# Moving the weight folds of a fused attention and gated-MLP kernel to 32x32 matrix tiles, and reordering its opening

## The chip, the core and the metric

The kernel runs on one core of a Trainium2 chip. A core has a matrix engine (TensorE, PE in the profile, with its weight loads listed as PEld), a vector engine (VectorE, DVE), an activation engine (ScalarE, ACT), a general engine (GpSimd, POOL) and a queue that issues most DMA transfers (SyncE, SP). Each engine works through its own list of instructions in order and waits on semaphores that the others raise. The metric is the device time of one execution in microseconds. The kernel before takes 2380.1 us (median of three runs, 2378.39 to 2380.84).

## The reference

`x` is 2048 tokens of 1024 values, normalised to `xn`. One branch is linear attention with 32 heads of 32 values and a learned feature map: a 32x32 matrix per head is applied to queries and keys before two softmaxes. The other branch is a SwiGLU MLP with 3584 hidden columns. Their product is added to `x`.

```python
qkv = (xn @ wqkv)                                   # q, k, v: 32 heads of 32
pq = einsum("bhsd,hdf->bhsf", q, w_phi)             # 32x32 per head
pk = einsum("bhsd,hdf->bhsf", k, w_phi)
phi_q = concat([softmax(pq), softmax(-pq)])         # the same for phi_k
kv = einsum("bhsf,bhsd->bhfd", phi_k, v);  z = sum_s phi_k
o = (phi_q @ kv) / (phi_q @ z + 1e-6)
s = o @ wo
h = silu(xn @ w1) * (xn @ w3);  g = silu(h @ w2)
out = x + s * g
```

## The kernel before

**Precision and products.** A matrix product in single precision is made as three products of values split into a high and a low part: `split` writes the high part as a cast on ACT (line 92) and the low part as a subtraction on DVE (line 93). Blocks are multiplied with a seven-product scheme (`ORDER`): each 2x2 block product takes seven products on sums of blocks, named A11, A12, S2, S1, S3, S4, A22 on the token side and B11, B21, T2, T1, T3, B22, T4 on the weight side. One such product is twelve matmuls of 128x512 and is here called a product; the gate and up projections of the MLP make 392 of them at line 598.

**The folds.** Since `w_phi` acts on each head of `q` and `k`, it can be multiplied into the key and query weights beforehand. Before, a fold is four f32 matmuls of 128x128 against `bd`, which holds the 32x32 matrices on the diagonal of 128x128 blocks (`fold`, line 247), a copy out of PSUM on ACT and a store to DRAM. There are 32 folds. Twelve of them (`FOLDS`) stand in the opening, twenty are placed as side work (`side_fold`).

**The opening.** The first 1024 tokens are loaded in two sets of four tiles. Each tile gets its mean and variance (`stats`, line 193, on DVE), the four deviations come from one square root on ACT (line 200) and a few small DVE operations (`rstd`), then `norm` (line 213), transposes on PE (`turn`, line 218), a copy out of PSUM on ACT (`raw_x`, line 223) and the split. All of this, in the order in which the code is written, is the order of each engine's list (`in_order`). The first four products are interleaved with it.

**The main loop and its side work.** `gate_up(step)` makes product number `step`, counted from 0; seven of them belong to one block of 128 hidden columns, `f`, and 28 such blocks to each half `tb` of the tokens. Around it stand the operands of later blocks and side work: normalising the other 1024 tokens (`side_x`), folds, the value and key weights (`side_kv`, which ends in 56 splits called `wkvo` and stores to `wkv_d`), `w2` (`side_w`). A function `room(step, cost)` gives DVE work a step: it adds the cost to a table of what each step already holds and moves on to the next step while the sum is over 2.55. Before, folds take no room.

**One hand-over of memory.** The side work's raw blocks come from the pool `xp` (14 buffers) and `bd` from `bdp`. At the first product of block `f = 25` (product 175) the code closes both and opens `spare` in the same place, and `fetch` (line 164, on SP) loads the second half's first operands, `op1A`, into it: eight DMAs. The code that issues the loads of `w1` and `w3` for the coming blocks (`b_load`, lines 256 and 257, tile `rw`, two buffers) puts them on the same SP list, and so are the stores of the hidden values (`h_d`) and of `wkvo`.

**The end.** After the last product of the MLP, `attend` (line 1336) and `out_half` (line 1351) work through 16 token tiles; `gate` (line 1053) applies the last silu on ACT.

Names that the later parts use: `bo` are split weight operands, `op0`/`op1` split token operands of the two halves, `u`, `h` hidden values, `wkv` raw blocks of `side_kv`, `consts` the statistics of the opening, `room_b` and `wr` the folds of the opening, `late_x` the second four token tiles.

Of the kernel before, what the change touches and what calls it, by code (L numbers as in the profile page):

```python
# [8 lines left out]
F = mybir.dt.float32  # L9
# [12 lines left out]
G = 8  # L22
# [7 lines left out]
def tile_kernel(ctx: ExitStack, tc: tile.TileContext, x, wkT, wqT, wv, wphi, wo, w1, w3, w2, out):  # L30
# [45 lines left out]
    wk_d = [[dram.tile([P, 512], F, name=f"wk_d{c}_{k}") for k in range(ND)] for c in range(2)]  # L76
    wq_d = [[dram.tile([P, 512], F, name=f"wq_d{c}_{k}") for k in range(ND)] for c in range(2)]
# [118 lines left out]
    def rstd(mv, sd=None):  # L196
# [3 lines left out]
        nc.scalar.activation(sd[:, 0], var, AF.Sqrt, bias=eps_t)  # L200
        yield sd
# [13 lines left out]
    def turn(half):  # L215
        pt = ps.tile([P, 4, P], F, name="pt", tag="tr", bufs=3)
# [33 lines left out]
    folds = [(wkT, k, c, wk_d[c][k]) for c in range(2) for k in range(ND)]  # L250
    folds += [(wqT, k, c, wq_d[c][k]) for c in range(2) for k in range(ND)]

    def b_load(f):

        rw = rwp.tile([P, 2, 2, 512], F, name="rw", tag="rw")
        nc.sync.dma_start(rw[:, 0], w1[f].rearrange("p (h k) n -> p h (k n)", h=2))
        nc.sync.dma_start(rw[:, 1], w3[f].rearrange("p (h k) n -> p h (k n)", h=2))
        return [rw[:, a, h] for a in range(2) for h in range(2)]

# [30 lines left out]
    phi_raw = flat(blk("phi")[:, :2]).rearrange("p (g f) -> p g f", f=DH)  # L290
    nc.sync.dma_start(phi_raw, wphi)
# [9 lines left out]
    for t in range(4):  # L301
        load_tile(t, quad("xt", F).rearrange("p u k t -> p u (k t)"))
        if t == 1:
            load_folds(2)
    rws = [b_load(0)]
    for t in range(4, 8):
        load_tile(t, late_x[:, t - 4])
    load_folds(4)
    rws.append(b_load(1))
# [76 lines left out]
    FIRST_PAIR = ((0, 0), (0, 1), (1, 0), (1, 1)) + tuple((f, j) for j in range(2, 7) for f in range(2))  # L386
# [107 lines left out]

    def side_fold(m, s0):
# [41 lines left out]
    for m in range(FOLDS, len(folds)):  # L537
        side_fold(m, FIRST_STEP + 48 + 11 * (m - FOLDS) // 2)
# [131 lines left out]
    for f in range(2):  # L670
        bos[0, f] = {}
        gens[0, f] = b_operands(rws.pop(0), bos[0, f], nc.gpsimd, held)
# [772 lines left out]
```

## Time and profile before

| | |
|---|---|
| runs, median (lowest, highest) | 2380.1 us (2378.39, 2380.84) |
| the profiled execution | 2381.62 us, its span 2379.8 us |
| PE busy | 2351.0 us, 99% |
| DVE, ACT, POOL busy | 1760.9, 910.1, 257.6 us |
| PE without work, 0 to 80 us | 15.9 us |
| PE without work, 80 to 2160 us | 7.6 us |
| PE without work, 2160 us to the end | 5.5 us |

The span is the time from the first to the last recorded instruction; the little that lies around it makes the time. A row of the timeline gives the start and the length in us, the engine, the line, the operation with its output and inputs, how many instructions were merged into the row, and in brackets how long the engine had been idle and who released it. A merged row's length is the time from its first start to its last end, and the last matmul's end reaches into the next row. An f32 matmul has two records in the trace. PEclk is the share of the full TensorE clock that the throttle granted.

### The profile page before, as it was taken

Reading aid. Unit: us, or ns where it says so; the run is one execution under the profiler, and the core shown is the slowest. Engines: PE = TensorE matmul, PEld = TensorE weight load, DVE = VectorE, ACT = ScalarE, POOL = GpSimd, SP = SyncE. Lnnn points to the kernel's source line nnn. Section 1 sums busy time; section 2 is a strip of 40 time slices with the busy share of each in tenths; the row PEclk is TensorE's granted clock in tenths of the full one; section 3 lists DMA queues with packets and bytes.
Section 4 is the critical chain, followed back from the end, with each engine's and each line's share of the span. In section 5 each row is a group of like instructions: output and inputs, shape, how many; then the busy total and the mean of one; then the engine's idle time right before and its main releaser. Section 6 shows DMA issues by size and latency. Waiting matters only on the chain.

```text
span 2379.8 us, 37194 instructions
## 1 busy us (share of the span) xinstructions
PE 2351.0 (99%) x14348; PEld 1934.9 (81%) x14348; DVE 1760.9 (74%) x2729; ACT 910.1 (38%) x1597; POOL 257.6 (11%) x243
## 2 busy tenths in 40 slices
PE   7999999999999999999999999999999999999999
PEld 6788888888888888888788888887888888887887
DVE  8877788765688888875566666777678888786775
ACT  6445454543444554543212222334433333352000
POOL 1000000000000000000000000331012222213562
PEclk9999999999999999999999999999999999999999
DMA  5446699985998888865977878986435653478763
GB/s 215 146 155 212 230 354 332 328 266 186 289 303 283 292 306 289 268 209 195 384 287 277 306 253 307 364 315 249 159 124 151 204 177 133 156 245 272 213 179 103
DMA packets 291472, 578.00 MB, mean 243 GB/s; under 512 B 24912, under 2 KB 140768, under 8 KB 288608
## 3 DMA queue, kind: packets, MB, share of 16 engines
q1 hardware_dynamic: 284960, 552.56, 68.5%
q10 hardware_dynamic: 6336, 23.07, 2.5%
q8 instruction: 113, 1.85, 0.3%
q14 instruction: 63, 0.52, 0.1%
HBM read 372.64 MB, written 202.91 MB: 242 GB/s over the span
## 4 chain that ended last, share of the span: by engine, by line
PE 93%; DVE 3%; DMA 2%; ACT 1%; SPq 1%; issue 0%; POOL 0%; DVEq 0%; ACTq 0%; POOLq 0%
PE bankb L598 24%; PE bankb L1199 13%; PE bankc L598 12%; PE pm L1351 8%; PE bankb L794 7%; PE bankc L1199 6%; PE banka L598 6%; PE bankc L794 3%; PE banka L1199 3%; PE bankb L861 3%; PE banka L794 2%; PE bankc L861 1%; PE po L1336 1%; PE pkv L779 1%; PE pw L247 1%; PE banka L861 1%
## 5 line engine op out<-in xcount | busy, mean ns | idle before, releaser
L93 DVE TENSOR_TENSOR bo<-rw,bo 128x512 fp32r<-128x512 f32 x336 | 230.9, 689 | 158.2 <-ACT bo L92 155.4
L1199 PE MATMUL bankb<-bo,as 128*128 128x512 f32 x960 | 235.2, 389 | 1.2 <-ACT acc L1205 1.2
L1199 PEld LDWEIGHTS bankb<-bo,as 128*128 128x128 f32 x960 | 180.2, 188 | 39.0 <-ACT acc L1205 1.6
L92 ACT CAST bo<-rw 128x512 fp32r<-128x512 f32 x336 | 206.5, 617 | 13.8 <-DMA w_d2B<-w2o 3.4
L598 PE MATMUL bankb<-op0S,bo 128*128 128x512 f32 x672 | 164.6, 394 | 1.9 <-ACT op0S L92 1.2
L598 PE MATMUL bankc<-op0S,bo 128*128 128x512 f32 x672 | 162.2, 391 | 0.0
L1351 PE MATMUL pm<-wos,oT 128*128 128x512 f32 x672 | 161.1, 394 | 0.9 <-DVE oT L1342 0.9
L598 PE MATMUL bankb<-op1S,bo 128*128 128x512 f32 x672 | 161.4, 389 | 0.6 <-ACT u L633 0.6
L598 PE MATMUL bankc<-op1S,bo 128*128 128x512 f32 x672 | 161.2, 389 | 0.0
L598 PE MATMUL bankb<-op0A,bo 128*128 128x512 f32 x672 | 159.7, 391 | 0.8 <-DVE bo L93 0.5
L771 POOL MEMSET ev<- 128x32 f32 x32 | 4.1, 129 | 1427.1 <-DMA xoA<-xo_d0A 1073.2
L1199 PE MATMUL bankc<-bo,as 128*128 128x512 f32 x624 | 158.4, 389 | 0.0
L598 PE MATMUL bankb<-op1A,bo 128*128 128x512 f32 x672 | 157.6, 390 | 0.0
L598 PEld LDWEIGHTS bankb<-op0S,bo 128*128 128x128 f32 x672 | 126.3, 190 | 29.0 <-ACT op0S L92 1.6
L1351 PEld LDWEIGHTS pm<-wos,oT 128*128 128x128 f32 x672 | 124.7, 188 | 29.5 <-DVE oT L1342 1.7
L598 PEld LDWEIGHTS bankb<-op1A,bo 128*128 128x128 f32 x672 | 125.9, 188 | 27.4 <-DVE u L641 1.3
L598 PEld LDWEIGHTS bankb<-op1S,bo 128*128 128x128 f32 x672 | 126.1, 188 | 27.1 <-ACT u L633 1.0
L598 PEld LDWEIGHTS bankc<-op1S,bo 128*128 128x128 f32 x672 | 126.1, 188 | 26.2
L598 PEld LDWEIGHTS bankb<-op0A,bo 128*128 128x128 f32 x672 | 125.2, 188 | 26.9 <-DVE bo L93 0.8
L598 PEld LDWEIGHTS bankc<-op0S,bo 128*128 128x128 f32 x672 | 125.4, 188 | 25.6
L1199 PEld LDWEIGHTS bankc<-bo,as 128*128 128x128 f32 x624 | 117.2, 188 | 24.4
L1213 DVE TENSOR_TENSOR acc<-bankb,acc 128x512 f32<-128x512 f32 x152 | 102.0, 685 | 31.1 <-PE bankb L1199 31.1
(262 smaller groups left out, 4343.8 us busy)
## 6 DMA issues: line engine op xcount, KB each, us to landing
rw<-in_w SPq DMA_DIRECT2D x112, 512.0 KB, 4.4
hr<-h_d SPq DMA_DIRECT2D x56, 512.0 KB, 4.8
h_d<-h SPq DMA_DIRECT2D x111, 256.0 KB, 5.4
xoS<-xo_d0S SPq DMA_DIRECT2D x44, 512.0 KB, 6.2
xoS<-xo_d1S SPq DMA_DIRECT2D x44, 512.0 KB, 6.1
xoA<-xo_d0A SPq DMA_DIRECT2D x33, 512.0 KB, 4.9
xoA<-xo_d1A SPq DMA_DIRECT2D x33, 512.0 KB, 4.4
e_d<-eq ACTq DMA_DIRECT2D x32, 512.0 KB, 6.3
```

The source lines that it names most:

```text
L92: nc.scalar.copy(hi, src)
L93: (by or nc.vector).tensor_sub(lo, src, hi.bitcast(F))
L247: nc.tensor.matmul(pw[:, g, :], wr[:, g], bd[:, 4 * c + g, :], start=True, stop=True)
L598: nc.tensor.matmul(bank[b], bos[tb, f][bn][:, w, k], ao[an][:, u, k], start=first and n == 0, stop=LAST[b] == an and n == 11, skip_group_c ...
L771: nc.gpsimd.memset(v[:, :, DH:], 1.0)
L779: nc.tensor.matmul(pkv[sl, m], e[:, m // 4, (m % 4) * P + 32 * h:(m % 4) * P + 32 * h + 32], v[:, 4 * (m % 4) + h], start=first and m == 0 ...
L794: nc.tensor.matmul(bank[b], xo[an][:, u, k], wb[bn][:, w, k], start=an in ("A11", "A12", "S1") and n == 0, stop=LAST[b] == an and n == 11, ...
L861: nc.tensor.matmul(bank[b], xo[an][:, u, k], wb[bn][:, w, k], start=an in ("A11", "A12", "S1") and n == 0, stop=LAST[b] == an and n == 11, ...
L1199: nc.tensor.matmul(bank[b], t[:, u, pos + k], bos[kb, bn, k][:, w], start=first and n == 0, stop=LAST[b] == an and n == 5, skip_group_chec ...
L1213: nc.vector.tensor_add(c, pb, c)
L1336: nc.tensor.matmul(po[32 * j:32 * j + 32, a, 64 * k:64 * k + 64], kvs[sl, j, c, k], et[sl, :, 4 * k + j], start=True, stop=True, skip_grou ...
L1351: nc.tensor.matmul(p, oTs[t, h][:, a, k], wos[c, 4 * h + k][:, b], start=n == 0, stop=n == 3 * ND - 1)
```

## The change

It has five parts. (1) The twenty folds of the side work become ten units. A unit takes the transposed weights of one group of four heads for all eight blocks of rows (two units: two groups, four blocks), 1024 values in each of 128 partitions, loaded into `bd`. It makes matmuls with the 32x32 matrix of a head as the stationary operand and 32 rows as the contraction: 16 of 256 columns, each in another 32x32 tile of the array, or 32 of 128 columns. They write four PSUM banks: three of the tag `tr` and one `banka`. DVE transposes each bank back in 32x32 blocks into `bd`, and one DMA stores it. Each pair of DVE transposes asks `room` for 0.7. (2) The four token tiles are loaded ahead of everything else, `w1` of two blocks ahead of both `w3`; twenty transposes of the raw tiles, whose results nobody reads, stand ahead of the first real ones. (3) The high and low parts of A11 and A12 are taken straight from PSUM, and the first four products run in the order A11 of blocks 0 and 1, then A12 of both. The folds of the opening stand behind the third product. (4) The order of the reads and statistics in the opening follows from that. (5) The silu of the last two tiles stands in the second and third turn of the last loop.

```diff
-    FIRST_PAIR = ((0, 0), (0, 1), (1, 0), (1, 1)) + ...
+    FIRST_PAIR = ((0, 0), (1, 0), (0, 1), (1, 1)) + ...
...
-    def rstd(mv, sd=None):
+    def rstd(mv, sd=None, between=None):
...
         nc.scalar.activation(sd[:, 0], var, AF.Sqrt, bias=eps_t)
+        if between:
+            between()
         yield sd
...
     for t in range(4):
         load_tile(t, quad("xt", F).rearrange("p u k t -> p u (k t)"))
-        if t == 1:
-            load_folds(2)
-    rws = [b_load(0)]
+    rws = [rwp.tile([P, 2, 2, 512], F, name="rw", tag="rw") for _ in range(2)]
+    b_part(rws[0], 0, 0)
+    phi_raw = early_z.rearrange("p (g f) -> p g f", f=DH)
+    nc.sync.dma_start(phi_raw, wphi)
+    load_folds(2)
+    b_part(rws[1], 1, 0)
     for t in range(4, 8):
         load_tile(t, late_x[:, t - 4])
+    for f in range(2):
+        b_part(rws[f], f, 1)
...
     def side_fold(m, s0):
-        wT, k, c, d = folds[m]
-        w = []
-        at(s0, lambda: w.append(load_w(wT, k, c)))
-        at(s0 + 5, lambda: w.append(flat(fold(w[0], c))), before)
-        at(s0 + 5, lambda: nc.scalar.copy(flat(w[0]), w[1]))
-        at(s0 + 7, lambda: nc.sync.dma_start(d, flat(w[0])))
+        w, banks = [flat(bd)], []
+        if m < 2:
+            gs_, nd = (4 + 2 * m, 5 + 2 * m), 4
+        else:
+            gs_, nd = (m - 2,), ND
...
+        def multiply():
+            banks.extend(ps.tile([P, 512], F, name="pf", tag="tr", bufs=3) for _ in range(3))
+            banks.append(ps.tile([P, 512], F, name="banka", bufs=BANKS["a"]))
+            for n, g in enumerate(gs_):
+                wn = w[0][:, 512 * n:512 * n + P * nd].rearrange("p (d k) -> p d k", d=nd)
+                for q in range(4):
+                    for j in (3, 0, 1, 2):
+                        sl = slice(32 * j, 32 * j + 32)
+                        nc.tensor.matmul(banks[j][32 * q:32 * q + 32, P * n:P * n + 32 * nd], phi_raw[sl, g], wn[sl, :, 32 * q:32 * q + 32],
+                                         start=True, stop=True, skip_group_check=True)
...
+        at(s0, multiply, before)
+        at_ = s0 - 1
+        for js in ((3, 0), (1, 2)):
+            at_ = room(at_ + 1, 0.7)
+            for j in js:
+                at(at_, lambda j=j: turn(j))
+        at(at_ + 2, store)
+        fold_free[0] = at_ + 4
...
-    for m in range(FOLDS, len(folds)):
-        side_fold(m, FIRST_STEP + 48 + 11 * (m - FOLDS) // 2)
+    for m, s0 in enumerate((52, 66, 87, 96, 108, 117, 129, 138, 150, 159)):
+        side_fold(m, s0)
...
+    nc.scalar.activation(sds[0][:, 1, :1], eps_t, AF.Sqrt)
+    warm = ps.tile([P, 512], F, name="banka", bufs=BANKS["a"])
+    for k in range(20):
+        nc.tensor.transpose(warm[:, :P], xs[2 + min(k // 8, 1)][k // 4 % 2][:, k % 4 * P:k % 4 * P + P], ident)
...
+    reads.append(gate_up(2))
+    first_folds(2)
+    first_copies(2)
+    stats(mvs[1], 0, xs[4])
+    stats(mvs[1], 1, xs[5])
+    reads[2]()
+    reads.append(gate_up(3))
     first_folds(4)
     load_folds(2)
     first_copies(2)
...
-    for j in range(2):
-        gate(len(pairs) - 1, j)
     prev = None
     for t in range(NT):
         p, last = out_half(t, 0), t + 1 == NT
         if t + 4 < NT:
             load_e(t + 4)
+        if 0 < t < 3:
+            gate(len(pairs) - 1, t - 1)
```

What this does to the lists of three engines is shown at three places. In these rows the number of a tile is kept, so that tiles of the same name can be told apart, and line numbers are those of the kernel that the row is from.

First, ACT in the opening, around the square root of the second four tiles (the row with `consts`). Before, the copies out of PSUM of the first two folds (`pw_473`, `pw_478`) stand ahead of it:

```order
L92 CAST op0A12_280<-xf_437 128x4x128
L333 COPY room_b_285<-pw_473 128x512
L333 COPY room_b_285<-pw_478 128x512
L200 ACTIVATE consts_274<-consts_274 128x4
L92 CAST bo_520<-rw_311 128x512
L92 CAST bo_523<-rw_311 128x512
L625 COPY h0_528<-bankb_439 128x512
```

Now four stand ahead of it. On PE the folds `pw_523` and `pw_528` follow the fourth product:

```order
L95 CAST bo_469<-rw_280 128x512
L682 COPY h0_472<-bankb_446 128x512
L343 COPY room_b_268<-pw_487 128x512
L343 COPY room_b_268<-pw_492 128x512
L343 COPY room_b_268<-pw_523 128x512
L343 COPY room_b_268<-pw_528 128x512
L203 ACTIVATE consts_257<-consts_257 128x4
L343 COPY wr_269<-pw_533 128x512
```

The square root has moved behind the copies of two folds that stand on PE behind the fourth product, where before it was behind folds that follow the second.

Second, DVE around the last of the 56 splits called `wkvo`. Before, it is `wkvo_4642`; the rows `L627` and `L641` around it read products 162 and 165, which belong to block 23:

```order
L93 TENSOR_TENSOR wkvo_4621<-wkv_4363,wkvo_4621 128x512
L627 TENSOR_TENSOR h0_4599<-banka_4601,h0_4599 128x512
L93 TENSOR_TENSOR bo_4639<-rw_4315,bo_4639 128x512
L93 TENSOR_TENSOR wkvo_4642<-wkv_4361,wkvo_4642 128x512
L93 TENSOR_TENSOR bo_4666<-rw_4479,bo_4666 128x512
L274 TENSOR_TENSOR rw_4479<-rw_4479,t2_4617 128x512
L93 TENSOR_TENSOR bo_4685<-rw_4479,bo_4685 128x512
L276 TENSOR_TENSOR rw_4479<-rw_4479,t2_4617 128x512
L641 TENSOR_TENSOR u1_4671<-bankb_4577,u1_4671 128x512
```

Now it is `wkvo_5123`; the rows `L698` and `L700` around it read products 179 and 180, which belong to block 25:

```order
L96 TENSOR_TENSOR wkvo_5103<-wkv_4808,wkvo_5103 128x512
L698 TENSOR_TENSOR u1_5085<-bankb_4992,u1_5085 128x512
L96 TENSOR_TENSOR bo_5120<-t2_5031,bo_5120 128x512
L96 TENSOR_TENSOR wkvo_5123<-wkv_4806,wkvo_5123 128x512
L700 TENSOR_TENSOR u0_5058<-bankc_5064,u0_5058 128x512
L701 TENSOR_TENSOR h0_5013<-h0_5013,u0_5058 128x512
```

The last split has moved two blocks down the list, past the point at which the code closes `xp`.

Third, the SP list around the loads of `op1A` into the memory of `xp`. Before, all stores of `wkvo` stand ahead of them, the last of them ten rows above the first row shown:

```order
L256 DMA rw<-in_w 128x1024
L257 DMA rw<-in_w 128x1024
L501 DMA wq_d_7_153<-wr 128x512
L164 DMA op1A_4882<-xo_d1A_94 128x8x128 x4
L164 DMA op1A_4887<-xo_d1A_95 128x8x128 x4
L556 DMA h_d_6_63<-h_4753 128x4x128
L256 DMA rw<-in_w 128x1024
L257 DMA rw<-in_w 128x1024
```

Now seven of these stores follow, two of them ahead of the next `rw`:

```order
L454 DMA wkv_d2T_121<-wkvo 256x1x512
L167 DMA op1A_4982<-xo_d1A_94 128x8x128 x4
L167 DMA op1A_4987<-xo_d1A_95 128x8x128 x4
L454 DMA wkv_d2B_115<-wkvo 256x1x512
L454 DMA wkv_d2B_116<-wkvo 256x1x512
L613 DMA h_d_6_63<-h_4839 128x4x128
L265 DMA rw<-in_w 128x1024 x2
L454 DMA wkv_d2T_117<-wkvo 256x1x512
L454 DMA wkv_d2T_118<-wkvo 256x1x512
```

The first of the four loads into `op1A_4982` waits for a semaphore of DVE that is raised by the split `wkvo_5123`; before, the first load waits for PE and for earlier DMAs.

More of the change, by code (lines that the diff above doesn't have):

```diff
@@ L700, in tile_kernel @@
     held.clear()
-    for t in range(1, 4):
+    for t in range(2, 4):
         stats(mvs[1], t, xs[4 + t])
@@ L704, in tile_kernel @@
     next(r1)
-    next(gens[0, 1])
-    next(gens[0, 1])
-    for do in held:
-        do()
-    reads[0]()
     first_copies(2)
-    reads[1]()
     load_folds(2)
@@ L732, in tile_kernel @@
     first_copies(2)
-    reads[3]()
     for f in range(2):
```

100 lines of the change are left out of this document (70 added, 30 removed).

## The prediction

> **What bounds the kernel now.** I read the page first, then busy time by stretches, then who PE waits for, and last the timeline of the places that the change touches. The page and the stretches (busy us of PE, PEld, DVE, ACT, POOL, then granted clock, DMA share, GB/s):
>
> ```profile
> span 2379.8 us, 37194 instructions
> PE 2351.0 (99%) x14348; PEld 1934.9 (81%) x14348; DVE 1760.9 (74%) x2729; ACT 910.1 (38%) x1597; POOL 257.6 (11%) x243
> ```
>
> ```profile
> 0.00:80.00 80.00, 64.06 (x330) 53.48 (x331) 68.71 (x129) 47.55 (x88) 8.38 (x16) 0.96 0.56 206
> 80.00:2160.00 2080.00, 2072.40 (x11159) 1709.32 (x11158) 1543.58 (x2434) 840.78 (x1475) 144.75 (x149) 1.00 0.73 250
> ```
>
> PE is the bound: it stands still for 16 us in the opening and 8 us in the 2080 us behind it. So a microsecond of PE work taken from the middle is a microsecond gained, and a wait that PE takes on there is lost in full. In the opening DVE is the busier of the two, 69 of 80 us. There a gain for PE counts only as far as DVE's list, and what feeds it, gets shorter.
>
> **The opening.** The rows that carry it:
>
> ```profile
> 9.79 1.29 DVE L193 BATCH_NORM_STATS2 st<-xt 128x6 f32<-128x512 f32 x2 [1.91 <-DMA xt<-in_x]
> 12.51 0.21 DVE L194 BATCH_NORM_AGGREGATE consts<-st 128x2 f32<-128x12 f32 x1
> 14.09 3.74 DVE L213 TENSOR_SCALAR xt<-xt,consts 128x512 f32<-128x512 f32 x8
> 17.75 1.28 DVE L93 TENSOR_TENSOR bo<-rw,bo 128x512 fp32r<-128x512 f32 x2
> 20.71 2.05 ACT L223 COPY xf<-pt 128x512 f32<-128x512 f32 x4
> 21.76 3.00 PE L598 MATMUL bankb<-op0A,bo 128*128 128x512 f32 x12
> 31.47 0.30 ACT L200 ACTIVATE consts<-consts 128x4 f32<-128x4 f32 x1 [0.60 <-DVE consts L194]
> 35.41 3.74 DVE L213 TENSOR_SCALAR late_x<-late_x,consts 128x512 f32<-128x512 f32 x8
> 47.86 6.13 PE L598 MATMUL bankb<-op0S,bo 128*128 128x512 f32 x24
> ```
>
> DVE lost 1.91 us on the third tile of x, which stood behind fold loads. With x first, four statistics of 1.45 us (1.29 and 0.21, overlapping a little) follow each other, and end near 10.5 instead of 12.7. The added split between the square root and the reciprocal (a cast of about 0.57, half of a pair of 1.14, and a subtraction of 0.64) takes back 1.1: the norms start near 13.0 instead of 14.1. High parts straight from PSUM let the first product begin near 16.5 and end near 19.5, five us earlier than now. But four products and their operands are not the end of the opening; the second four tiles are. Following DVE's list from 13.0: norms 1.9, four low parts 2.5, one weight split 0.6, norms 1.9, another split 0.6 gives 20.5; the A12 low parts wait half a us for their transposes and end at 23.5. The next split needs a cast that ACT has behind four A12 casts, a copy and four raw copies (2.05 for four): DVE stands for about 2 us, to 25.6. Two statistics bring 28.5, and only then comes the addition that empties the one `banka`, so the fourth product starts at 29.8 and ends at 32.5. Behind it are the folds whose copies stand ahead of the square root on ACT: it runs near 35, where DVE has its last statistics at 32.7, and the late norms start near 36.3 instead of 35.4. One addition of 0.6 now stands ahead of the sums. So the first S2 product comes at about 49.1 instead of 47.9: the five us are gone before 48.
>
> The clock pulls the other way:
>
> ```profile
> 11.00:14.30 3.30, 0.02 (x1) 0.00 (x0) 2.69 (x11) 1.79 (x5) 0.00 (x0) 1.00 1.03 421
> 14.30:17.70 3.40, 3.01 (x14) 3.01 (x15) 3.40 (x8) 1.58 (x4) 0.00 (x0) 0.50 1.02 414
> 17.70:21.00 3.30, 1.75 (x16) 1.47 (x14) 3.04 (x6) 3.28 (x7) 0.00 (x0) 1.00 1.06 413
> 62.10:65.50 3.40, 3.40 (x9) 2.62 (x10) 3.40 (x7) 1.10 (x3) 0.00 (x0) 0.50 0.32 133
> 65.50:69.00 3.50, 3.50 (x17) 2.90 (x16) 3.50 (x7) 3.50 (x8) 0.00 (x0) 1.00 0.00 0
> ```
>
> An idle stretch is followed by 3.4 us at half clock, which costs up to 1.7 us of PE work. The second such loss (at 62) may or may not fall on the changed kernel: between +1.2 with it and -0.8 without it I take +0.5, with -3 to +3 as ends. The twenty added transposes run while PE has nothing else; their cover is the wait for x, and they cost nothing. The Trainium skill (TensorE: Matmul & The Clock Gate, Part 4) says that transposes do not count as PE activity for the clock; by that the twenty would leave the first real transposes at half clock, some 1 us more in the sum. The trace speaks against it: the stretch 14.3 to 17.7 holds transposes alone, and the clock is full right behind it.
>
> **The folds.** A fold in the side work, and the nearest rows for a unit:
>
> ```profile
> 229.53 1.05 PE L247 MATMUL pw<-bd,wr 128*128 128x128 f32 x8
> 230.34 2.98 PE L598 MATMUL bankb<-op0S,bo 128*128 128x512 f32 x12
> 2172.29 0.86 PE L1336 MATMUL po<-acc,kvs 64*32 64x64 f32 x64
> 2173.08 0.98 PE L1351 MATMUL pm<-late,oT 128*128 128x512 f32 x3
> L1123 PE MATMUL us<-early_z,consts x2: 377/377/377, 2043.2 to 2043.4; 128*128 128x256 f32 x2
> 2170.07 2.37 DVE L1179 STREAM_TRANSPOSE acc<-acc 128x1024 f32<-128x1024 f32 x2
> ```
>
> From start to next start a fold takes 0.81 us, so twenty are 16.2 us, all on PE's path. The `po` rows show 32 small f32 matmuls (64 records) in 8 tiles of the array in 0.79 us, 0.025 each. One f32 matmul with 256 columns streams for about 0.4 us (the two records of `us` start 0.2 apart), so 64 columns take 0.1, and 32 of them one after another 3.2: eight tiles overlapped four times. For a unit (16 of 256 columns, or as many columns in all) that gives 16 x 0.4 / 4 = 1.6 as the upper end. The lower end is issue alone with one stream on its tail, 16 x 0.025 + 0.2 = 0.6. I take 0.9, nearer the lower end, since in `po` issue, not streaming, seems to have set the pace. Ten units: 9.0, a gain of 7.2 (0.2 to 10). The Trainium skill (TensorE: Matmul & The Clock Gate, Part 3) gives a speedup of 10.6 for 16 such tiles; by it a unit would stream for an estimated 0.6 us, the gain would be 10 and the sum 6. No run here shows 16 tiles.
>
> The twenty fold copies leave ACT, which is idle 60% of the time: nothing. DVE gets 40 transposes of 256 columns (0.3 each by the row of 1024 columns) and as much in the two narrow units, 12 us, with a quarter of its time free; a unit holds `banka` and all three `tr` banks until then. I book 0.5 for PE (0 to 2).
>
> **What the units push aside.** `room` now gives 20 slots of 0.7 to the folds, and the 56 `wkvo` splits move down DVE's list, the last from among the reads of products 162 to 165 to just ahead of that of product 180. The code closes `xp` at product 175. The load of `op1A` into its memory must wait for that split, and it is SP that waits. Behind it stand stores and `rw`, the weights of block 27. The rows of this place now:
>
> ```profile
> 512.55 0.69 DVE L93 TENSOR_TENSOR wkvo<-wkv,wkvo 128x512 fp32r<-128x512 f32 x1
> 538.12 11.90 SPq L164 DMA_DIRECT2D op1A<-xo_d1A  x8
> 550.11 2.27 SPq L556 DMA_DIRECT2D h_d<-h  x1
> 553.22 0.45 SPq L257 DMA_DIRECT2D rw<-in_w  x1
> 559.86 0.69 DVE L643 TENSOR_TENSOR u<-bankc,u 128x512 f32<-128x512 f32 x1 [1.43 <-PE bankc L598]
> 567.05 0.68 DVE L128 TENSOR_TENSOR rw<-rw 128x512 f32<-128x512 f32 x1
> 570.74 0.59 ACT L633 COPY u<-bankb 128x512 f32<-128x512 f32 x1 [0.50 <-PE bankb L598]
> 573.26 2.88 PE L598 MATMUL bankb<-op0S,bo 128*128 128x512 f32 x12
> ```
>
> ```profile
> rw<-in_w SPq DMA_DIRECT2D x2, 512.0 KB, 5.3
> op1A<-xo_d1A SPq DMA_DIRECT2D x8, 512.0 KB, 6.9
> 541.00:550.00 9.00, 9.00 (x42) 7.44 (x41) 5.67 (x9) 2.21 (x4) 0.00 (x0) 1.00 0.98 287
> ```
>
> Today 25 us lie between the last split (513.2) and the first load (538.1). The read at 559.86 is that of product 180; the split now comes about there, at 560 on today's clock, so SP stands some 22 us longer. From the first load to the landing of the second `rw` (553.22 and 5.3 us) took 20.4 us; two `wkvo` stores of 512 KB more are 2.5 us at the 421 GB/s of the opening's row: `rw` lands near 583. DVE wants it at 567.05. DVE then stands, behind it an addition that ACT's silu needs, behind that the copy at 570.74 which frees the bank for product 186, due at 573.26. From the sum at 567.05 to the end of that copy are 4.3 us: product 186 starts near 587, a stall of 14 us. If all 6.6 MB moved at those 421 GB/s, instead of 287 GB/s for `op1A`, `rw` would land near 578 and the stall be 9; with 287 for all of it, 16 to 17. I take 13.5, nearest to the transfers as they ran here (9 to 17). Such an idle stretch of PE ends at half clock: 1.7 more (0 to 3.4).
>
> **The last silus.**
>
> ```profile
> 2166.57 0.59 ACT L1341 CAST oT<-po 128x512 fp32r<-128x512 f32 x1 [0.27 <-PE po L1336]
> 2167.05 2.01 ACT L1053 ACTIVATE acc<-acc 128x1024 f32<-128x1024 f32 x2
> 2173.18 0.59 ACT L1341 CAST oT<-po 128x512 fp32r<-128x512 f32 x1 [4.12 <-PE po L1336]
> ```
>
> Nobody waits behind them: ACT idles for 4.12 us afterwards. Moving them is worth 0.
>
> **The sum.** +0.5 (opening) - 7.2 (folds) + 0.5 (DVE) + 13.5 (stall) + 1.7 (clock) + 0 = +9.0 us. The profiled execution took 2381.6 us, 1.5 above the median 2380.1, and would become 2390.6; for the median that is 2389.
>
> **The rivals.**
> *The block is hidden.* If the split came five products earlier, or the waiting load did not hold up those behind it, `rw` would be in time. For it speaks that every `rw` now lands 8 us or more before its sum (558.5 against 567.05). Against it: SP issues in order, and the lists put `rw` behind the load. Then the sum is 9.0 - 15.2 = -6.2: 2374, faster. It decides at a split done before 544 on today's clock, that is 567 less 23.
> *The stall is short and the units cheap.* 9 us of stall, 0.6 a unit: 9.0 - 4.5 - 3 = +1.5, 2381.6, the same. For it speaks the rate of 421 GB/s elsewhere; against it the 287 for this very load.
> *The tiles do not overlap.* A unit streams 16 x 0.4 = 6.4 us, ten 64 instead of 9: 2444. `po` speaks against it, but its streams are four times shorter.
>
> **How the numbers follow.** My forecast 0.73, the hidden block 0.09, the short stall 0.12, no overlap 0.06. A change under 0.2% (4.8 us) can't be told from none: slower above 2384.9, faster below 2375.3. Some of the forecast's own spread falls in the middle; that gives faster 0.09, same 0.14, slower 0.77. The range leaves out no overlap and the hidden block: its lower end 2377 lies just under a stall of 9 with units at 0.6 and the opening at -3 (9.0 - 4.5 - 3 - 3.5 = -2, so 2378); its upper end 2398 is stall 17 with units at 1.3 and 1.5 lost in the opening (9 + 3.5 + 4 + 1 = 17.5).
>
> **What would show it.** Each unit takes 0.6 to 1.6 us on PE between two products. The first product starts near 16.5, the late norms after 35, the square root of the late tiles behind a fold's copy. Near 570 to 585 PE stands 9 to 17 us, the chain of releasers going through ACT and DVE to the DMA of `rw`, and SP's own longest wait, over 20 us, is ahead of `op1A`. I am wrong if PE runs through there, if a unit takes over 2 us, or if the first S2 product starts before 46.

## The result and the profile after

| | before | changed |
|---|---|---|
| median of four runs | 2379.24 us | 2389.74 us |
| lowest, highest | 2378.26, 2380.84 | 2389.33, 2394.62 |
| profiled execution, its span | 2381.62, 2379.8 us | 2389.33, 2387.5 us |

The ratio is 1.0048 (95% interval 1.0031 to 1.0066): slower by about half a percent, where the forecast was 2389. The rows of the changed kernel that answer to those shown of before, first the page, then the stretches (busy us of PE, PEld, DVE, ACT, POOL; clock, DMA share, GB/s), then who waited longest on PE and on SP's queue:

```profile
span 2387.5 us, 37640 instructions
PE 2347.3 (98%) x14592; PEld 1924.1 (81%) x14592; DVE 1774.7 (74%) x2777; ACT 898.5 (38%) x1577; POOL 257.4 (11%) x243
```

```profile
0.00:80.00 80.00, 65.83 (x346) 55.62 (x347) 66.66 (x126) 46.49 (x87) 8.77 (x16) 0.98 0.55 202
80.00:2160.00 2080.00, 2059.76 (x11351) 1689.65 (x11350) 1554.55 (x2478) 825.47 (x1449) 143.56 (x148) 1.00 0.73 249
569.20:586.30 17.10, 5.89 (x14) 4.63 (x15) 5.72 (x9) 4.24 (x8) 0.00 (x0) 0.50 1.06 377
```

```profile
PE bankb L655 <- ACT u L690: 14.0, 1, 14.0
```

```profile
SPq L167 <- DVE wkvo L96: 24.3, 1, 24.3
```

PE has less to do than before (2347.3 against 2351.0 us) and takes longer. From 80 to 2160 us it stands still for 20.2 us instead of 7.6. One wait makes up 14.0 of them, and SP has a wait of 24.3 us that it did not have. Line numbers have moved: products are now L655, splits L95 and L96, the sum of `rw` L131, the load of `op1A` L167, that of `rw` L265, the square root L203, fold copies L343, the unit's matmuls L532.

The place of the stall, in the timeline of the changed kernel:

```profile
553.53 0.69 DVE L96 TENSOR_TENSOR wkvo<-wkv,wkvo 128x512 fp32r<-128x512 f32 x1 [1.79 <-ACT wkvo L95]
554.25 10.67 SPq L167 DMA_DIRECT2D op1A<-xo_d1A  x8
568.17 1.88 SPq L265 DMA_DIRECT2D rw<-in_w  x2
576.69 0.69 DVE L131 TENSOR_TENSOR rw<-rw 128x512 f32<-128x512 f32 x1 [14.35 <-DMA rw<-in_w]
578.74 0.63 ACT L688 ACTIVATE h<-h 128x512 f32<-128x512 f32 x1 [17.13 <-DVE h L684]
580.41 5.49 PE L655 MATMUL bankb<-op0S,bo 128*128 128x512 f32 x12 [14.03 <-ACT u L690]
585.70 3.21 PE L655 MATMUL bankc<-op0S,bo 128*128 128x512 f32 x12
```

It is read from below. Product 186 waits for ACT's copy of `u`, which stands behind the silu, which waits for DVE, which waits for `rw`. That load is issued at 568.17, behind the eight loads of `op1A`, and the first of these is issued at 554.25, 0.03 us after the end of the last `wkvo` split. The products are 5.49 and 3.21 us long where 2.88 is usual: PE is at half clock until 586.3.

The opening, in the same view:

```profile
17.30 3.29 PE L655 MATMUL bankb<-op0A,bo 128*128 128x512 f32 x12 [0.68 <-ACT op0A L738]
30.35 3.00 PE L655 MATMUL banka<-op0A,bo 128*128 128x512 f32 x12 [0.73 <-ACT room_b L343]
35.65 0.30 ACT L203 ACTIVATE consts<-consts 128x4 f32<-128x4 f32 x1
35.98 0.18 DVE L207 RECIPROCAL consts<-consts 128x4 f32<-128x4 f32 x1 [2.96 <-ACT consts L203]
49.71 0.50 PE L655 MATMUL bankb<-op0S,bo 128*128 128x512 f32 x1
```

The first product comes 4.5 us earlier than before and the fourth 9.4 (39.74 before), but the first S2 product 1.85 us later.

Where the 7.7 us between the two profiled spans come from, by the starts of the 392 products in both traces: the opening +1.0 (constant from product 11 to 51), folds and units -8.8, four small waits for DVE +0.7, the stall +14.2, half clock behind it +2.9, a wait of before at 650 us that is gone -0.9. That is +9.1 at the end of the MLP. The stages behind it give 1.5 back. The medians differ by 10.5 us, 2.8 more than these two executions.

### The profile page after: what moved, and what is told of

The parts are those of the page before. It is cut to its first block, busy times and chain, and to the rows that moved or that the text cites. A ratio compares the mean times of both kernels' runs of the same rounds, so it can differ in the third digit from the quotient of the medians.

```text
span 2387.5 us, 37640 instructions
## 1 busy us (share of the span) xinstructions
PE 2347.3 (98%) x14592; PEld 1924.1 (81%) x14592; DVE 1774.7 (74%) x2777; ACT 898.5 (38%) x1577; POOL 257.4 (11%) x243
## 4 chain that ended last, share of the span: by engine, by line
PE 94%; DVE 2%; DMA 2%; SPq 1%; ACT 0%; issue 0%; POOL 0%; DVEq 0%; ACTq 0%; POOLq 0%
PE bankb L655 25%; PE bankb L1280 13%; PE bankc L655 12%; PE pm L1432 8%; PE bankb L875 7%; PE bankc L1280 6%; PE banka L655 6%; PE bankb L942 4%; PE bankc L875 3%; PE banka L1280 3%; PE bankc L942 2%; PE banka L875 2%; PE po L1417 1%; PE banka L942 1%; PE pkv L860 1%; DMA op2T<-wkv_d1T 1%
## 5 line engine op out<-in xcount | busy, mean ns | idle before, releaser
L96 DVE TENSOR_TENSOR bo<-rw,bo 128x512 fp32r<-128x512 f32 x336 | 230.8, 688 | 153.6 <-ACT bo L95 153.2
L95 ACT CAST bo<-rw 128x512 fp32r<-128x512 f32 x336 | 206.7, 618 | 17.6 <-DMA w_d2B<-w2o 3.1
L655 PE MATMUL bankb<-op0S,bo 128*128 128x512 f32 x672 | 166.5, 398 | 14.8 <-ACT u L690 14.0
L655 PE MATMUL bankc<-op0S,bo 128*128 128x512 f32 x672 | 163.6, 392 | 0.3 <-DVE op0S L96 0.3
L655 PEld LDWEIGHTS bankb<-op0S,bo 128*128 128x128 f32 x672 | 128.4, 192 | 42.8 <-ACT u L690 14.4
L655 PE MATMUL bankb<-op1S,bo 128*128 128x512 f32 x672 | 161.2, 389 | 0.0
L655 PE MATMUL bankc<-op1S,bo 128*128 128x512 f32 x672 | 161.2, 389 | 0.0
L655 PE MATMUL bankb<-op0A,bo 128*128 128x512 f32 x672 | 159.2, 391 | 0.7 <-ACT op0A L738 0.7
L655 PE MATMUL bankb<-op1A,bo 128*128 128x512 f32 x672 | 157.6, 390 | 0.0
L655 PEld LDWEIGHTS bankc<-op0S,bo 128*128 128x128 f32 x672 | 125.4, 188 | 30.1 <-issue 2.9
L655 PEld LDWEIGHTS bankb<-op1A,bo 128*128 128x128 f32 x672 | 125.9, 188 | 27.4 <-DVE u L698 1.3
L655 PEld LDWEIGHTS bankb<-op0A,bo 128*128 128x128 f32 x672 | 125.2, 188 | 27.9 <-ACT op0A L738 0.9
L655 PEld LDWEIGHTS bankc<-op1S,bo 128*128 128x128 f32 x672 | 126.1, 188 | 26.2
L655 PEld LDWEIGHTS bankb<-op1S,bo 128*128 128x128 f32 x672 | 126.1, 188 | 26.2
```

Source lines behind the costliest of these rows:

```text
L95: nc.scalar.copy(hi, src)
L96: (by or nc.vector).tensor_sub(lo, src, hi.bitcast(F))
L655: nc.tensor.matmul(bank[b], bos[tb, f][bn][:, w, k], ao[an][:, u, k], start=first and n == 0, stop=LAST[b] == an and n == 11, skip_group_c ...
```

## The experiments

All are compared with the kernel before, run beside them; its median was between 2380.2 and 2381.2 us.

### Is it the reservations that make the stall?

Two rivals: the twenty `room` reservations, which only move DVE's list, or the units themselves. One run takes the reservations out of the changed kernel:

```diff
-            at_ = room(at_ + 1, 0.7)
+            at_ = at_ + 1
```

> The changed kernel, its units unchanged, but they reserve no room in DVE's list: the last wkvo split goes back to where it stood before the change. Theory (the reservations push the splits, op1A waits for the last one on SP, and rw of block 27 stands behind it): PE's 14.2 us stall ahead of product 186 and the 2.9 us of half clock behind it go, 2389.7 - 17.1 = 2372.6 us; SP's longest wait is no longer at op1A. Rival (the units themselves, their matmuls, transposes, loads or stores, make SP or DVE late): the stall stays, 2389 to 2390 us.

Another puts them alone into the kernel before:

```diff
         side_fold(m, FIRST_STEP + 48 + 11 * (m - FOLDS) // 2)
+    for s0 in (52, 66, 87, 96, 108, 117, 129, 138, 150, 159):
+        at_ = s0 - 1
+        for _ in range(2):
+            at_ = room(at_ + 1, 0.7)
```

> The kernel before, with its own folds and opening, but with the twenty reservations of 0.7 in the planner's table at the units' steps, and not one instruction added: only the order of DVE's list changes. Theory: the last wkvo split lands at the reads of products 179 to 180 again, so the stall of some 14 us and the 2.9 us of half clock come alone, 2379.2 + 17 = 2396 us. Rival (the units cause the stall): no change, 2379 us.

Without them: 2375.6 us, ratio 0.998 (0.997 to 0.9989). They alone: 2392.4 us, ratio 1.0054 (1.0039 to 1.0069). So the stall comes and goes with twenty entries in a table, with not one instruction added. The timeline of the kernel before with the reservations:

```profile
557.43 0.68 DVE L93 TENSOR_TENSOR wkvo<-wkv,wkvo 128x512 fp32r<-128x512 f32 x1
558.14 10.16 SPq L164 DMA_DIRECT2D op1A<-xo_d1A  x8
579.88 0.69 DVE L128 TENSOR_TENSOR rw<-rw 128x512 f32<-128x512 f32 x1 [9.97 <-DMA rw<-in_w]
583.60 5.19 PE L602 MATMUL bankb<-op0S,bo 128*128 128x512 f32 x12 [9.64 <-ACT u L637]
```

The stall is 9.6 us and not 14. Here `op1A` goes out behind the last split but one (557.43 and 0.68 make 558.11), 3.7 us ahead of the end of the last one (561.8); in the changed kernel it waited for the last. From the first load to the sum of `rw` it takes 21.7 us, against 22.4 there. The two differences make up the 4.4 us by which the stall is shorter.

### Is it SP's queue, or a late weight for another reason?

The changed kernel with its reservations, but the loads of `op1A` issued at product 178, behind `rw` of block 27:

```diff
-            for m in range(2):
-                early.update(fetch(tb + 1, m))
+            if tb:
+                for m in range(2):
+                    early.update(fetch(tb + 1, m))
         for late in load_at.get(step, ()):
             rws.append(b_load(late[1]))
+        if (tb, f, j) == (0, NF - 3, 3):
+            for m in range(2):
+                early.update(fetch(tb + 1, m))
```

> The changed kernel with its reservations, so that the wkvo splits are as late as in it, but the two loads into the memory of xp (op1A and its neighbour) are issued at product 178, behind the load of rw of block 27, instead of at product 175. Theory (SP issues in order, and rw is late only because it stands behind the waiting load): rw lands in time, the stall goes, 2372.6 us, though SP still waits for the split. Rival (rw is late because DVE's or the DMA engines' work has grown, not for its place behind op1A): 2389 to 2390 us.

2374.6 us, ratio 0.9977 (0.9968 to 0.9987). The split is as late as in the changed kernel, SP waits for it (6.0 us), and nobody minds:

```profile
546.55 0.81 SPq L265 DMA_DIRECT2D rw<-in_w  x2
552.69 0.68 DVE L96 TENSOR_TENSOR wkvo<-wkv,wkvo 128x512 fp32r<-128x512 f32 x1
553.40 10.33 SPq L167 DMA_DIRECT2D op1A<-xo_d1A  x8
561.04 0.68 DVE L131 TENSOR_TENSOR rw<-rw 128x512 f32<-128x512 f32 x1
```

`rw` goes out 6.9 us ahead of `op1A` and its sum has no wait. So the order on SP is the link. Both this run and the one without reservations stay 2 to 3 us above the 2372.6 expected. Their traces gain 15.6 us on the changed kernel at the end of the MLP, not 17.1: the one without reservations meets new waits of 0.46 us at 357 and of 1.17 at 599, and this one keeps the DVE waits and had an opening 1.0 us longer.

### What are the units worth, and does their order matter?

The kernel before with the units alone, no reservations, its own opening and last silus. It takes over the new `side_fold` with its buffers, its steps and the layout of `wqT`; two places of the edit:

```diff
-    for m in range(FOLDS, len(folds)):
-        side_fold(m, FIRST_STEP + 48 + 11 * (m - FOLDS) // 2)
+    for m, s0 in enumerate((52, 66, 87, 96, 108, 117, 129, 138, 150, 159)):
+        side_fold(m, s0)
...
-        "wqT": lay(wqkv[:, :D]),
+        "wqT": wqkv[:, :D].T.reshape(G, P, D),
```

> The kernel before, with its own opening and last silus, in which only the twenty side folds are replaced by the ten units, without reservations. Theory: the folds cost PE 20 x 0.91, the units 8 x 0.87 + 2 x 1.24, and waits for DVE 0.7: -18.2 + 9.4 + 0.7 = -8.1, so 2379.2 - 8.1 = 2371.1 us, and the new opening, which it lacks, costs about 1 us against it. Rival (the new opening gains and the units cost more than they look): no faster than 2375 us.

2379.0 us, ratio 0.9991 (0.9982 to 1.0): no gain, and 8 us above the expectation. But at the end of the MLP the trace is 7.64 us ahead of before (0.8 of it was there before the first unit), where the terms gave 8.1. Of the 5.5 us that it loses behind that, 1.8 go in the key, value and query products and 3.7 in the last stage, which is followed up below.

The sixteen matmuls of a unit in another order, on the kernel without reservations:

```diff
-                for q in range(4):
-                    for j in (3, 0, 1, 2):
+                for j in (3, 0, 1, 2):
+                    for q in range(4):
```

> The changed kernel without reservations, the sixteen matmuls of a unit in another order: the four that share 32 rows of the array come one behind another (column group innermost) instead of four that lie in four different groups of rows. Theory A (a stream occupies its group of 32 rows, and matmuls are issued in order): one stream of 256 columns takes some 0.4 us, four of a group follow each other, a unit takes 5 us or more instead of 0.87, ten units add 40 us: some 2416 us. Theory B (issue sets the pace, any sixteen tiles overlap): 0.87 a unit as before, 2375.6 us.

2373.6 us, ratio 0.9968 (0.9955 to 0.9981). The groups of the unit's matmuls in the changed kernel and in this one (ns least, median, most):

```profile
L532 PE MATMUL pf<-bd,early_z x288: 267/374/398, 187.9 to 492.4; 32*32 32x256 f32 x96, 32*32 32x128 f32 x48
```

```profile
L532 PE MATMUL pf<-bd,early_z x288: 267/374/399, 187.9 to 492.9; 32*32 32x256 f32 x96, 32*32 32x128 f32 x48
```

A unit costs PE 0.74 us where it stands and 0.13 in the next product, in both orders: theory B, and matmuls that share their 32 rows overlap as well as others. Against the prediction's estimate of 6.4 us for sixteen streams one behind another, 0.87 is 7.4 times faster. The Trainium skill (TensorE: Matmul & The Clock Gate, Part 3) has 10.6 for sixteen such tiles with 512 columns; this kernel's units, with what they cost their neighbour, stay under it.

### What holds the opening back?

The prediction put the loss on the square root behind the fold copies. On the kernel without reservations two copies were moved behind it:

```diff
     first_folds(4)
     load_folds(2)
-    first_copies(2)
...
     next(r1)
-    first_copies(2)
+    first_copies(4)
     load_folds(2)
```

> The changed kernel without reservations, and in its opening the square root of the late tiles stands on ACT ahead of two more copies of folds instead of behind them. Theory (the opening loses its early start because that square root waits behind copies of folds that follow the fourth product): DVE's idle time of about 3 us ahead of the reciprocal shrinks to under 1, the first S2 product starts some 2 us earlier than the 48.8 us of the same kernel without this edit, and 1 to 2 us stay to the end: about 2374 us. Rival (DVE's own list, not ACT, sets the S2 product, or the copies that now come later hold PE's folds): no difference, 2375.6 us.

2373.5 us, ratio 0.997 (0.9957 to 0.9982). In its timeline:

```profile
32.22 0.30 ACT L203 ACTIVATE consts<-consts 128x4 f32<-128x4 f32 x1 [2.85 <-DVE consts L197]
32.55 0.18 DVE L207 RECIPROCAL consts<-consts 128x4 f32<-128x4 f32 x1 [0.37 <-ACT consts L203]
47.02 0.49 PE L655 MATMUL bankb<-op0S,bo 128*128 128x512 f32 x1
```

DVE's idle 2.96 us are 0.37, and the S2 product comes 1.7 us earlier than in the same kernel without the edit (48.76). That it is the edit is seen best in a later run which also has it (the last below): its fourth product starts at 30.35, as in the changed kernel, and its S2 product at 47.91 instead of 49.71.

The twenty transposes that nobody reads, taken out:

```diff
-    for k in range(20):
-        nc.tensor.transpose(warm[:, :P], xs[2 + min(k // 8, 1)][k // 4 % 2][:, k % 4 * P:k % 4 * P + P], ident)
```

> The changed kernel without reservations and without the twenty transposes at the start of the opening, whose result nobody reads. Theory of the prediction (they engage the clock for the first real transposes, but the opening's end is set by DVE): the granted clock is 0.5 for 3.4 us from the first real transposes, the first product starts 1 to 2 us later, the first S2 product within 1 us of 48.8, 2375 to 2376.5 us. Rival (transposes do not count as work for the clock): the stretch from 13 us shows the same clock with and without them, and nothing moves.

2379.9 us, ratio 0.9998 (0.9988 to 1.0008). Its opening, and then that of the kernel with them, which has no reservations either:

```profile
13.18 3.65 PE L223 MATMUL pt<-ident,xt 128*128 128x128 f32 x16 [13.18 <-DVE xt L218]
17.50 4.86 PE L655 MATMUL bankb<-op0A,bo 128*128 128x512 f32 x12 [0.68 <-ACT op0A L738]
```

```profile
7.05 4.50 PE L750 MATMUL banka<-ident,xt 128*128 128x128 f32 x20 [7.05 <-DMA xt<-in_x]
13.22 2.03 PE L223 MATMUL pt<-ident,xt 128*128 128x128 f32 x16 [1.68 <-DVE xt L218]
```

Both statements on record fail. Three kernels that have the transposes start their first product about as late as this one (17.27, 17.30 and 17.32 us, here 17.50) and the first S2 product at 49.66, 49.71 and 49.83; here it comes at 51.47, 1.7 us later. The delay is not absorbed, since the square root waits for copies behind the fourth product. And the rival is out: in the seven kernels that have the twenty transposes, with no small matmuls behind them, the first product takes 3.29 to 3.62 us, though PE has run nothing but transposes until then; without the twenty it takes 4.86. The sixteen transposes ahead of that product are another matter. They took 2.03 us in two of the seven, and 3.29 to 3.54 in the other five, little less than the 3.65 without. The changed kernel is one of the five:

```profile
13.16 3.47 PE L223 MATMUL pt<-ident,xt 128*128 128x128 f32 x16 [1.65 <-DVE xt L218]
```

The Trainium skill (TensorE: Matmul & The Clock Gate, Part 4) says that transposes do not count as PE activity; the 2.03 us and the lengths of the first products speak against it. The other part of this run's loss is in the last stage.

### Why does the last stage lose 3 us in two of the kernels?

In the kernel with the units alone, and in that without the twenty transposes, PE stands still at the start of the last stage. The timelines of the two:

```profile
2158.98 1.71 PE L1385 MATMUL po<-acc,kvs 64*32 64x64 f32 x128
2163.80 7.75 PE L1400 MATMUL pm<-wos,oT 128*128 128x512 f32 x21 [3.10 <-DMA wos<-wo_d]
```

```profile
2159.46 1.70 PE L1414 MATMUL po<-acc,kvs 64*32 64x64 f32 x127
2164.18 0.24 PE L1414 MATMUL po<-acc,kvs 64*32 64x64 f32 x1 [3.02 <-issue]
```

The first names a load, but the second stops ahead of the last of 128 records of `po`, at a matmul that waits for nothing ("issue"). The transfers of the first kernel from 2161.4 to 2162.5 us, in the standstill, by queue (packets, MB, share):

```profile
q1 hardware_dynamic: 119, 0.43, 98.6%
q8 instruction: 1, 0.02, 5.5%
```

One packet is on the queue q8, which in this kernel carried 115 packets of 16 KB for 29,475 recorded PE instructions: 256 instructions each. Counted from 0 at the start of the trace, PE stopped at instruction 24,001 in both kernels, which is 193 modulo 256. So I took it that PE had run out of instructions, and moved its stream against the blocks by 32 small matmuls in the opening:

```diff
     first_folds(2)
+    pad = ps.tile([P, 512], F, name="banka", bufs=BANKS["a"])
+    for k in range(32):
+        nc.tensor.matmul(pad[:32, :64], ident[:32, :32], ident[:32, :64], start=True, stop=True)
     first_copies(1)
```

> The kernel with the units alone (the one before, its own opening, no reservations) came out at 2379.0 where 2371 was expected. Its trace is 7.6 us ahead of the kernel before until the last stage and loses 5.7 us there: PE stands 3.0 us ahead of its first output product, at half clock behind that, and a 16 KB packet on the queue of PE's instructions moves at 2161.43, in the middle of the standstill. Here 32 small matmuls (32x32 by 64 columns, into a bank that nobody reads) are added to the opening where PE idles, which does nothing but move PE's instructions against those 16 KB blocks by 64. Theory (PE ran out of instructions, because a block's end fell on the 128 quick matmuls po): the stall moves or goes, 2373 to 2374 us. Rival (the wait is for the load of wos that the profile names, or comes of ACT's order there): the stall stays at the same product, 2379 us.

2377.8 us, ratio 0.9984 (0.9975 to 0.9993): the standstill is gone from the last stage, and so are the 5.7 us that it took there (3.1 and half clock behind it). The time expected is missed by 4 us all the same: the profiled execution, 2376.1 us, was 1.7 us behind its counterpart at the end of the MLP, 1.2 of them from the opening, and the median lies 1.7 above it. By their medians (2379.0 and 2377.8, intervals that overlap) the two kernels are not told apart; what this run shows is in its trace.

The opposite, 51 such matmuls of 8 columns in the kernel before:

```diff
     first_folds(2)
+    pad = ps.tile([P, 512], F, name="banka", bufs=BANKS["a"])
+    for k in range(51):
+        nc.tensor.matmul(pad[:32, :8], ident[:32, :32], ident[:32, :8], start=True, stop=True)
     first_copies(1)
```

> The kernel before and nothing else changed, but 51 small matmuls (32x32 by 8 columns, nobody reads them) in the opening's idle time: they add 204 instructions to PE's stream, so that the 256 instructions of the first po run make up exactly one 16 KB block, and the first pm is number 193 modulo 256, as in the two kernels that stood still there. Theory (a block is asked for when the one ahead of it begins, and 256 po instructions run in 1.7 us, faster than a block comes through full queues): PE stands some 3 us ahead of the first pm and runs at half clock behind it, 2380.2 + 5 = 2385 us. Rival (that standstill is a late load of wos, which only the changed kernels have): no standstill there, 2380 us.

2383.0 us, ratio 1.001 (1.0001 to 1.002): slower by half of what was expected, and without a standstill at the first `pm`, where the block had come 4 us ahead of `po`. Of the 4.1 us by which its profiled execution is longer, 2.0 come from the opening, where the small matmuls took 5.6 us and held up the first transposes; so the median says nothing of the blocks. But in the trace PE now stands where before had no such stop, at a later `po`, instruction 24,769, again 193 modulo 256:

```profile
2205.83 0.72 PE L1339 MATMUL po<-acc,kvs 64*32 64x64 f32 x48
2208.70 0.35 PE L1339 MATMUL po<-acc,kvs 64*32 64x64 f32 x16 [2.15 <-issue]
```

The changed kernel has one too, at 25,025 (193 modulo 256):

```profile
2210.22 0.48 PE L1417 MATMUL po<-acc,kvs 64*32 64x64 f32 x33
2212.10 0.46 PE L1417 MATMUL po<-acc,kvs 64*32 64x64 f32 x31 [1.40 <-issue]
```

So the block's end sets where PE can stop. Whether it does is told by the packets' own times in the traces, one packet to a block. Seven of the fourteen kernels have such a stop, and in each of the seven PE goes on 1.24 to 1.46 us after the end of the packet that is due there. At the other 1584 block ends of the fourteen traces that packet had ended 1.55 us or more before PE came. So PE did wait for its instructions. What makes a packet late stays open: the data queues were busy to 98.6% in the case above, but only to 48 and 44% around two other stops, and to 108% where the kernel without reservations passed instruction 25,025 without one.

### The last silus, and two tries at a better kernel

The two silus back in their old place, on the kernel without reservations:

```diff
     for c in range(2):
         attend(0, c)()
+    for j in range(2):
+        gate(len(pairs) - 1, j)
...
-        if 0 < t < 3:
-            gate(len(pairs) - 1, t - 1)
```

> The changed kernel without reservations, the last two silus back where they stood before the change, ahead of the loop over the output tiles. Prediction's term 0: ACT has several us free there, 2375.6 us either way. Rival (the moved silus free ACT for the casts oT and PE's products come earlier): 1 us or more slower, with PE waiting for ACT ahead of a pm.

2372.2 us, ratio 0.9969 (0.9956 to 0.9982), not told apart from 0.998 (0.997 to 0.9989) with them moved. From the end of the down projection to the end of the span it gains 2.0 us on before, and so does the run with `op1A` later, which has them moved: the term is 0.

The square root moved, no reservations, and 22 small matmuls at the start of the opening, to shift the blocks:

```diff
+    pad = ps.tile([P, 512], F, name="banka", bufs=BANKS["a"])
+    for k in range(22):
+        nc.tensor.matmul(pad[:32, :8], ident[:32, :32], ident[:32, :8], start=True, stop=True)
     for t in range(4):
         stats(mvs[0], t, xs[t])
```

> The units without reservations, the square root of the late tiles ahead of the fold copies, and 22 small matmuls (32x32 by 8 columns, into a bank that nobody reads) in the opening's idle time, which add 88 instructions to PE's stream and so move it against the 16 KB blocks to where the trace of the kernel with 32 such matmuls showed no standstill in the last stage. The kernel with the square root moved was 9.06 us ahead of the one before at the end of the gate and up products and lost 1.96 of it in the last stage, at an instruction whose number is 193 modulo 256. Theory: that standstill goes, 2373.5 - 2 = 2371.5 us, 9 us under the kernel before. Rival (the blocks have nothing to do with it): 2373.5 us, with the standstill still ahead of the second or third po.

2374.8 us, ratio 0.9977 (0.9968 to 0.9986), 3 us above the expectation. The last stage gains its 2.0 us, without a stop. The opening loses 3.8 against the kernel with the square root moved:

```profile
11.55 2.51 PE L753 MATMUL banka<-ident 32*32 32x8 f32 x44
13.99 3.67 PE L223 MATMUL pt<-ident,xt 128*128 128x128 f32 x16
18.34 5.27 PE L655 MATMUL bankb<-op0A,bo 128*128 128x512 f32 x12 [0.68 <-ACT op0A L738]
```

The twenty transposes are followed by small matmuls, and then the real ones take 3.67 and a product 5.27 us. The 3.67 alone would prove little, with 3.29 to 3.54 in five kernels without small matmuls; the 5.27 stand against 3.29 to 3.62. The same 22 ahead of the opening's last fold, where PE waits for ACT:

```diff
+    pad = ps.tile([P, 512], F, name="banka", bufs=BANKS["a"])
+    for k in range(22):
+        nc.tensor.matmul(pad[:32, :8], ident[:32, :32], ident[:32, :8], start=True, stop=True)
     first_folds(1)
     first_copies(2)
```

> The kernel with the square root moved and no reservations, and the 22 small matmuls not at the start of the opening but ahead of its last fold, where PE waits 1.6 us for ACT. Placed at the start they had taken the clock away from the first transposes and the first product (3.67 us for sixteen transposes instead of 2.03, 5.27 for the product instead of 3.3) and so cost the opening 3.9 us, while the last stage did gain its 2 us. Theory: the opening as without them, some 9 us ahead of the kernel before at the end of the gate and up products, no standstill at an instruction 193 modulo 256 in the last stage: 2380.4 - 9.5 = 2371 us. Rival (small matmuls cost as much wherever they stand, or the last stage stands still elsewhere): 2373.5 us or more.

2375.7 us, ratio 0.998 (0.9971 to 0.9989): the rival's 2373.5 or more. The first S2 product comes at 47.91 instead of 50.90, but at the end of the MLP the trace is 6.8 us ahead of before and not 9: 0.9 of the difference lies in the opening and 0.5 in a wait for DVE at 337, the rest was not traced. The key and value products then lose 1.6 us at their start, and PE stands 0.6 us at instruction 24,769. So three of the kernels without the stall (2372.2, 2373.5, 2373.6) beat the kernel before by about 0.3%. They are not told apart from each other, nor from those at 2374.6 to 2375.7.

## The prediction, step by step

*The block pushed aside* (+13.5): right in mechanism and size. The stall measured 14.2. The prediction had product 186 start near 587 on the clock of before; 580.41 and the 7.04 us that the changed kernel was ahead there make 587.45. The transfers took 22.4 us from the first load to the sum, where 22.9 had been worked out. The reservations and the order on SP were each shown by a run; the late split and `rw` stand in the timelines.

*The clock behind it* (+1.7): mis-sized, 2.9 measured. I had taken 3.4 us of half clock, as in the rows of the opening; after 14 us of idleness it lasted 5.9 us beyond the restart.

*The folds* (-7.2): -8.8. A fold was worth 0.91, not 0.81, since the product behind it was 0.10 slower too; a unit cost 0.87, two of them 1.24, where 0.9 had been taken. The waits for DVE (+0.5) were 0.7; its transposes of 256 columns took 0.41 us, where 0.3 had been read from a row of another kind.

*The opening* (+0.5): +1.0 in the profiled execution. The order of events came as written: the first product early (17.30 against 16.5), the square root behind a fold copy, the late norms at 36.99 (36.3), the S2 product at 49.71 (49.1). That the square root is the cause was shown by moving it. The step on the twenty transposes was in part wrong. It rejected half clock in the first real transposes, and here they ran at about half speed (3.47 us for sixteen, 1.91 for the next sixteen), as in five of seven kernels. And it valued the twenty at nothing, where they bring the first S2 product 1.7 us forward.

*The last silus* (0): right. *What the sum left out*: the later stages gave 1.5 back, most of it in the query products, by waits that no term covers; inside it stands the 1.40 us of waiting for instructions. That the forecast of 2389 met a median of 2389.7 is in part luck: the terms came to +10.0 instead of +9.0, with 1.6 too little gain on the folds against 2.6 too little loss on the others, and 2.4 us that stood in no term came back (0.9 at 650 us and these 1.5).

Of the rivals, the hidden block (2374) is what came out whenever the stall was taken away: 2375.6 and 2374.6. The tiles overlap; the short stall did not come.

## What to carry to other kernels

A planner's reservation is a change like any other: follow the last item that it pushes until the memory that this item reads is to be reused, and look at what stands behind the load that must then wait, on a queue that issues in order. When a kernel's time moves by 2 to 5 us without a reason in its own terms, count PE's instructions at the place where it stands with "issue" ahead of it, in this kernel and in a shifted one, before explaining it by a load that the profile names, and look when the packet with its instructions came.

## What was not expected of the hardware

PE's instructions come in blocks of 16 KB on a DMA queue of their own, 256 at a time (113 packets for 29,026 recorded instructions in the kernel before, 115 for 29,516 in the changed one). Seven kernels stopped at an instruction 193 modulo 256, to within one, for 0.5 to 3.1 us, all in the last stage, where PE runs 64 or 128 records of `po` at 0.013 us each. The seven others did not, though in four of them instruction 25,025 stands at the same place of the same `po` as in the changed kernel: a block's end is where it can happen, and a late packet makes it happen. The kernel without the twenty transposes, 40 instructions shorter in the opening, took 4.5 us longer in the last stage than the same kernel with them, some 2150 us later.

The opening differs from execution to execution: in five kernels the same lines started their first product at 16.03, 17.27, 17.30, 17.32 and 18.36 us, with the S2 product at 48.76 to 50.74. In the first the sixteen transposes ran in 2.03 us, in the others in 3.29 to 3.50, and in the last `x` came 1.0 us later. Of 2 us between two such kernels nothing should be read unless their first products start alike. Small matmuls did not keep the clock. In the kernel with 32 of 64 columns they fill the first of these two stretches, and the clock of the second is half (PE, PEld, DVE, ACT, POOL, clock, DMA share, GB/s):

```profile
11.36:14.77 3.41, 3.41 (x63) 3.41 (x63) 2.84 (x10) 1.92 (x5) 0.00 (x0) 1.00 1.03 420
14.77:18.18 3.41, 3.41 (x20) 3.24 (x18) 3.41 (x9) 1.45 (x3) 0.00 (x0) 0.50 1.02 414
```
